# Another third PSUM bank, a batch begun one step sooner and merged operand sums in a fused attention and MLP kernel

## The chip, the cores and the metric

The kernel runs on one core of a Trainium2 chip. The metric is the device time of one execution in microseconds (us). A profiled execution also gives a span, from its first to its last instruction, and a trace of every instruction with its start and end. Engines are named as in the profile: PE (TensorE, matmuls), PEld (its weight loads), DVE (VectorE), ACT (ScalarE), POOL (GpSimd) and SP (SyncE); POOL and SP mostly issue DMAs here.

## The reference

Eight batches of grouped attention (16 query heads, 4 key and value heads, 384 tokens, head size 64) feed a residual MLP with affine scales in place of norms:

```python
scores = (1/sqrt(64)) * q @ k.T                     # per head; k, v shared by 4 query heads
x   = softmax(scores) @ v                           # heads side by side: [8, 384, 1024]
tok = einsum('ts,bsd->btd', w_tok, alpha1 * x + beta1)
u   = x + lam * tok
a2  = alpha2 * u + beta2
out = u + lam * (relu(a2 @ w_ch1) @ w_ch2)          # w_ch1 1024x4096, w_ch2 4096x1024
```

## The kernel before

**Stages.** Batches 0 and 1 are computed one by one (`main`). Batches 2 to 7 go through the MLP two at a time in three stages (`pair(0)`, `pair(1)`, `pair(2)`). A stage multiplies the two batches' stacked 2x2 block matrix by the blocks of the weights with a seven-product scheme in place of eight: sums and differences of blocks are formed on DVE, and seven products `o` are made and added up. The first product of a stage (first matmul by `w_ch1`, L723) runs over 8 groups `g` of 14 small products each, in the order of `SEQ1`; a small product is four matmuls of 128x384 into a bank X, Y or Z. The second product (second matmul by `w_ch2`, L785, tile C) runs over the seven `o` in the order 1, 2, 6, 5, 3, 7, 4 (`PLACE2`), and in each over three token tiles `ms` with 16 matmuls of 128x512.

**Steps.** Both products are generators. The second product yields after every four matmuls: 12 steps for each of the first six `o`, and 12 for `o` = 4, which is made in two halves `h` of eight matmuls for each `ms`. So it has steps 0 to 83; `o` = 7 has steps 60 to 71, `o` = 4 has 72 to 83, and its third token tile is first touched in step 76. A plan, written out by hand at the end of the kernel, holds functions under (stage, product, step); what stands under step u is issued right after the matmuls of step u. Every engine runs its instructions in this order.

**The work beside the second product.** In the first two of the three stages, the attention and token mixing of the next two batches, c and c+1, run in the gaps of the second product. `side(b)` returns a table of steps. Per batch it has six `scores3` (three score tiles each, L279, and three `exp` on ACT, L288; the last `exp` of some is put off until after the next value product), and for each of eight parts p (128 columns, two heads) a value product `av` (L315; then DVE divides by the row sums, L320 and L323, and makes the operand of the token product, L328 and L330) and a token product `tok` (L340; then DVE adds it to x, L347, and scales it, L351). `tok_flip` is `tok` and then a spill of x to `out` by DMA (L243) and a transposition by DMA (L362). For the parts 5, 6 and 7 of the second batch the transposition is made by PE in `turn` instead (L427) and copied out by ACT (L429). Batch c's table is used as it is, batch c+1's with 39 added to each step.

**PSUM.** `share_banks` gives out the eight banks anew for each product. In the second product two banks are `acc`, two buffers for C, and the other six are three score tiles of two banks each, sc0, sc1 and sc2. `three()` hands these out in rotation: scores, value products, token products and turns take one each, and each has to wait until the tile's last user is read out. The last product of a stage, `o` = 4, has three C tiles open at once in the first two of the three stages, since its two halves go over all `ms`: two in `acc`, the third in a score tile (`c_banks`). From then on `three()` skips that tile (`held`). In the last stage there are no score tiles in use, and C takes banks of them for its third token tile throughout and for the end of `o` = 7.

**DVE's other work there.** C is read out by L817, L819, L822 and L824 (the last for `o` = 7), and scaled by L687 (`scaled`, called by `flush` at certain steps) ahead of an accumulating store to `out` by POOL (L516). For the next stage DVE makes differences of weight blocks (`sum_w1`, L620 and L625), the operand sums of four parts (`sums_a`, three operations each, L585 to L587, of opb(0) to opb(5), planned at steps 74, 77, 80 and 82) and, in the next stage's first group, opb(6) (L740). The second small operand opb(0) is first used by the third small product (`o` = 7, bank Y), opb(6) by the tenth (`o` = 3, bank X).

**Weights.** A ring of six slots holds blocks of 512 KB; `load_w1` (POOL, L185) and `fetch` (SP, L636) fill a slot when the last step that reads it frees it. Two more slots lie in `pad`.

Of the kernel before, what the change touches and what calls it, by code (L numbers as in the profile page):

```python
# [12 lines left out]
def kernel(  # L13
# [22 lines left out]
    f32 = mybir.dt.float32  # L36
# [4 lines left out]
    ADD = mybir.AluOpType.add  # L41
# [7 lines left out]
    P = 128  # L49
# [145 lines left out]

    def three():
        if pairs:
            pairs["turn"] = (pairs["turn"] + 1 + (pairs["turn"] == 0 and pairs["held"])) % 3
            return pairs["sc%d" % pairs["turn"]].tile([P, 2, 4, P], f32, tag="sc", name="sc", bufs=1)
        return threes[0].tile([P, 2, 4, P], f32, tag="sc", name="sc", bufs=3)  # L200

# [27 lines left out]
    def side(b):  # L229
# [201 lines left out]
        if not first:  # L431


            turns = {}
            if b == 1:
                turns = {4: [(to_all, 3, 0, 0), (to_all, 3, 1, 1), (load_row_set, 1, 1, 0), (load_row_set, 2, 0, 1)],
                         8: [(k_transpose, 0)], 12: [(to_all, 1, 0, 2), (to_all, 1, 1, 0), (load_row_set, 2, 1, 0)],
                         16: [(scale_beta,)], 20: [(to_all, 2, 0, 1), (to_all, 2, 1, 0)],
                         24: [(q_transpose, 0, 2, "av")], 28: [(k_transpose, 2)]}
                for i in range(3):  # L440
                    turns[32 + 4 * i] = [(q_transpose, 2 + 2 * i, 2, "av")]
            if (b - NPL) // 2 > 0:
                at = {}

                def put(k, *m):
                    at.setdefault(k, []).append(m)

                for j in range(6):
                    put((0, 6, 12, 21, 26, 31)[j], scores3, j, j in (2, 5))
                for p in range(NP):  # L450
                    put((4, 10, 14, 18, 24, 29, 33, 35)[p], av, p)
                    put((8, 15, 17, 22, 27, 32, 36, 38)[p], tok_flip, p)
                    if by_pe(p):
                        put((36, 39, 41)[p - NP + 3], turn, p)
                return turns, at
            return turns, {
                0: [(scores3, 0)], 4: [(av, 0)], 6: [(scores3, 1)], 8: [(tok_flip, 0)], 11: [(av, 1)],
                13: [(scores3, 2, True)], 15: [(av, 2)], 16: [(tok_flip, 1)], 18: [(tok_flip, 2)], 19: [(av, 3)],
                21: [(scores3, 3)], 23: [(tok_flip, 3)], 25: [(av, 4)], 27: [(scores3, 4)], 29: [(tok_flip, 4)],
                31: [(av, 5)], 33: [(scores3, 5, True)], 35: [(av, 6), (tok_flip, 5)], 37: [(av, 7)],  # L460
                38: [(tok_flip, 6)], 41: [(tok_flip, 7)],
                **{39 + 4 * i - i // 2 * 2: [(turn, p)] for i, p in enumerate((5, 6, 7)) if by_pe(p)}}
# [118 lines left out]

    tt = nc.vector.tensor_tensor

    def sums_a(j):
        tt(out=opb(2)[:, j], in0=opb(0)[:, j], in1=opb(1)[:, j], op=ADD)  # L585
        tt(out=opb(0)[:, j], in0=opb(3)[:, j], in1=opb(0)[:, j], op=SUB)  # L586
        tt(out=opb(5)[:, j], in0=opb(2)[:, j], in1=opb(3)[:, j], op=SUB)  # L587

    kept, tb = {}, {}

# [79 lines left out]
    def pair(i):  # L670
# [82 lines left out]
                    tt(out=hid[:, ts, 3], in0=hid[:, ts, 2], in1=hid[:, ts, 1], op=ADD)  # L753
                yield 0
        finish(slice(NH - 2, NH))
        share_banks("acc", "sc1", "sc0", "sc2")
        acc = pairs["acc"]

        def c_banks(ms):
            return [(0, 512, pairs["sc1"].tile([P, 2, 512], f32, tag="sc", name="C", bufs=1)[:, 0] if ms == NST - 1 else  # L760
                     acc.tile([P, 512], f32, tag="acc", name="C", bufs=2))]

        X = [c_banks(ms) if last else None for ms in range(NST)]
# [2 lines left out]
        for k, o in enumerate(PLACE2):  # L766
            whole = not last and o != 4
            for h in range(1 if whole else 2):
                for ms in range(NST):
                    if o == 4 and not last and 1 < 3 * h + ms < 5:  # L770
                        sum_w1(0, (5, 7, 6)[3 * h + ms - 2])
                    if last and (o, h) in ((6, 1), (7, 0)):
                        (lift_end if o == 7 else begin_end)(ms)
                    if last and (o, h, ms) == (7, 0, NST - 1):
                        X[ms] = [(c0, c1, pairs[sc].tile([P, 2, 512], f32, tag="sc", name="C", bufs=1)[:, 0, :c1 - c0])
                                 for sc, c0, c1 in (("sc0", 0, 384), ("sc2", 384, 512))]
                    if whole:
                        X[ms] = [(0, 512, acc.tile([P, 512], f32, tag="acc", name="C", bufs=2))]
                    elif not last and h == 0:
                        X[ms] = c_banks(ms)  # L780
                        pairs["held"] = ms == NST - 1
                    upto = NH if whole else 8 * h + 8
                    for (c0, c1, x), t in ((c, t) for c in X[ms] for t in range(8 * h, upto)):
                        slot, rhs = w2_slots[i, 4 * k + t // 4], w2_at[i, 4 * k + t // 4]
                        nc.tensor.matmul(out=x, lhsT=hid[:, t, LEFT2[o], ms * P:(ms + 1) * P],  # L785
                                         rhs=rhs[:, t % 4 * 512 + c0:t % 4 * 512 + c1],
                                         start=((not last or o in (1, 6, 7)) and t == 0), stop=(t == NH - 1),
                                         skip_group_check=True)
                        if t % 4 == 3 and ms == NST - 1 and c1 == 512 and not (o == 4 and slot >= RING):
                            free(slot)  # L790
                        if last and o == 4 and t == NH - 1:
                            e, v = ends[ms][:, c0:c1], spare(ms).bitcast(f32)[:, c0:c1]
                            tt(out=v, in0=x, in1=lam_t[:, c0:c1], op=MUL)
                            tt(out=e, in0=e, in1=v, op=ADD)
                            nc.sync.dma_start(out=by_tok(out[b0 + 1])[:, ms, c0:c1], in_=e)
                        if t % 4 == 3 and t < upto - 1 and c1 == 512:
                            q = 4 * ms + t // 4
                            if whole and o in (2, 6) and q in (2, 5, 8, 10):
                                sums_hid(o, (2, 5, 8, 10).index(q))
                            if t % 8 == 3:  # L800
                                flush(1)
                            yield 1
                    if k == ms == h == 0:
                        pad_free[:] = [RING, RING + 1]
                        pump()
                    if (whole or h == 1) and not (last and o == 4):
                        if o in (1, 6, 5):
                            q = ((1, 6, 5).index(o) * NST + ms) * 512
                            snap[o, ms] = snaps[:, q:q + 512]
                        else:  # L810
                            bb, dw = where[o]
                            t = snap[1, ms] if o == 7 else spare(ms).bitcast(f32)
                        for c0, c1, x in X[ms]:
                            if o == 1:
                                nc.scalar.copy(out=snap[o, ms], in_=x)
                            elif o in (6, 5):
                                tt(out=snap[o, ms], in0=x, in1=snap[1 if last or o == 6 else 6, ms], op=ADD)  # L817
                            elif o == 2 and last:
                                tt(out=t, in0=x, in1=lam_t[:, :512], op=MUL)  # L819
                            else:  # L820
                                base = {2: 1, 3: 1 if last else 5, 7: 5, 4: 6}[o]
                                tt(out=t[:, c0:c1], in0=x, in1=snap[base, ms][:, c0:c1], op=ADD)  # L822
                            if o == 7 and not last:
                                tt(out=snap[6, ms], in0=x, in1=snap[6, ms], op=ADD)  # L824
                        if o not in (1, 6, 5):
                            later.append((scaled, o, b0 + bb, ms, dw, t))
                    if last and o in (2, 6) and (h, ms) in ((0, 1), (0, 2), (1, 0), (1, 1)):
                        sums_hid(o, [(0, 1), (0, 2), (1, 0), (1, 1)].index((h, ms)))
                    yield 1
# [4 lines left out]
    with tc.manual_schedule(engines=order):  # L834
# [162 lines left out]
        for i in range(NB - 1):  # L997
# [5 lines left out]
            put_all(ps, 1, side(c)[1])  # L1003
            for u, f, h in ((10, flip_q, 0), (17, flip_k, 0), (18, flip_q, 2), (28, flip_q, 4), (33, flip_k, 2), (33, flip_q, 6)):
                put(ps, 1, u, f, c + 1, h, 2)
            put_all(ps, 1, side(c + 1)[1], lambda u: u + 39)
            for j, u in ((1, 77), (0, 74), (2, 80), (3, 82)):
                put(ps, 1, u, sums_a, j)
        for ps in range(NPL + NB):
            done = [0, 0]  # L1010
            for second in main(ps) if ps < NPL else pair(ps - NPL):
# [43 lines left out]
```

## Time and profile before

| | us |
|---|---|
| median of 3 runs (747.96 to 750.38) | 748.25 |
| the profiled execution | 747.4 |
| its span | 745.6 |
| second product of the first paired stage | 316.60 to 419.68 |
| second product of the second paired stage | 492.83 to 595.91 |
| PE busy in each of these two (103.08 long) | 99.47 |
| DVE busy in the same | 77.65 and 77.43 |
| DMA engines' share in the same | 0.96 and 0.95 |

The times inside the span count from its first instruction. "Busy" is the union of an engine's instructions; the end of a matmul is modelled, so that a gap on PE is best counted from the start of one instruction to the start of the next. A name such as `xr<-sc,xr` is what an instruction writes and what it reads.

### The profile page before, as it was taken

The page shows a single profiled execution, that of the slowest core. Times are in us where ns is not written, and L with a number is a line of the kernel's source. Part 1 is how long each engine was busy: PE and PEld are TensorE (multiplying, and loading weights), DVE is VectorE, ACT ScalarE, POOL GpSimd, SP SyncE. Part 2 cuts the span into 40 slices and gives each one's busy share as a digit, 9 for nine tenths or more (in the row PEclk, how much of TensorE's full clock was granted, in tenths as well). Part 3 has the DMA queues.
Part 4 walks back from the last instruction along what each step waited for, and adds up shares of the span by engine and source line. Part 5 has one row for each costly group of instructions (what it writes and reads, how often), then busy time and mean ns, then how long its engine had stood idle before and what let it go on. Part 6 is the DMA issues. An engine that isn't in the chain of part 4 may idle for free.

```text
span 745.6 us, 14462 instructions
## 1 busy us (share of the span) xinstructions
PE 728.5 (98%) x5710; PEld 418.7 (56%) x5769; DVE 522.2 (70%) x1010; ACT 319.1 (43%) x458; POOL 163.2 (22%) x211
## 2 busy tenths in 40 slices
PE   8999999999999999999999899999999899999997
PEld 5856555566555566655555466655555456654444
DVE  7763366577677899749778977747958887762344
ACT  7622341433342666653334366663343266660000
POOL 9434220420000232301021433110002231000011
PEclk9999999999999999999999999999999999999999
DMA  9999999999998999998979999999979998936975
GB/s 185 193 201 200 207 216 165 182 190 203 212 275 244 187 219 211 250 258 201 275 191 246 151 195 173 195 195 206 269 232 185 195 181 114 154 120 235 285 216 102
DMA packets 218017, 151.32 MB, mean 203 GB/s; under 512 B 88660, under 2 KB 197060, under 8 KB 217948
## 3 DMA queue, kind: packets, MB, share of 16 engines
q0 software_dynamic: 120304, 64.60, 65.9%
q1 hardware_dynamic: 97100, 85.39, 41.8%
q8 instruction: 45, 0.74, 0.4%
q10 hardware_dynamic: 544, 0.39, 0.2%
q14 instruction: 24, 0.20, 0.1%
HBM read 154.84 MB, written 38.27 MB: 259 GB/s over the span
## 4 chain that ended last, share of the span: by engine, by line
PE 85%; DVE 7%; DMA 4%; issue 2%; POOL 1%; ACT 0%; DVEq 0%
PE C L785 25%; PE X L723 16%; PE ch L569 10%; PE h L531 10%; PE Y L723 8%; PE sc L279 4%; PE Z L723 4%; PE sc L315 3%; PE sc L340 3%; DMA q_raw<-in_q_dram 2%; DMA ops<-a 1%; DVE xr L323 1%; DVE a1f L328 1%; DVE xr L347 1%; DVE hT L822 1%
## 5 line engine op out<-in xcount | busy, mean ns | idle before, releaser
L288 ACT ACTIVATE es<-sc 128x1024 bf16<-128x1024 f32 x126 | 121.4, 1023 | 163.8 <-PE sc L279 152.6
L785 PE MATMUL C<-w,arena 128*128 128x512 bf16 (+2 forms) x777 | 179.8, 373 | 6.8 <-DVE xr L347 5.0
L785 PEld LDWEIGHTS <-arena 128*128 128x128 bf16 x1040 | 94.8, 98 | 105.7 <-issue 10.3
L728 ACT ACTIVATE hT<-X,bias 128x384 f32<-128x384 f32 x144 | 83.7, 582 | 61.0 <-PE X L723 53.8
L723 PEld LDWEIGHTS <-w 128*128 128x128 bf16 x768 | 75.2, 98 | 50.0
L185 POOL DMA_DIRECT2D w<-in_moe_w_ch_dram x68 | 61.4, 911 | 131.7 <-PE X L723 73.8
L569 PE MATMUL ch<-arena,hT 128*128 128x512 bf16 x366 | 87.9, 379 | 1.0 <-issue 0.3
L516 POOL DMA_DIRECT2D out_dram<-hT x33 | 28.5, 863 | 260.6 <-DVE hT L687 161.1
L531 PE MATMUL h<-ops,w 128*128 128x384 bf16 (+1 forms) x480 | 83.3, 327 | 1.6 <-DVE hT L542 1.4
L723 PEld LDWEIGHTS <-pad 128*128 128x128 bf16 x576 | 56.3, 98 | 38.0 <-issue 0.8
L723 PE MATMUL X<-ops,w 128*128 128x384 bf16 x384 | 70.3, 326 | 0.0
L723 PE MATMUL X<-ops,pad 128*128 128x384 bf16 x384 | 70.3, 326 | 0.0
L531 PEld LDWEIGHTS <-w 128*128 128x128 bf16 x480 | 45.4, 98 | 31.2 <-issue 2.4
L569 PEld LDWEIGHTS <-hT 128*128 128x128 bf16 x384 | 34.8, 98 | 36.8 <-issue 2.5
L785 PE MATMUL C<-pad,arena 128*128 128x512 bf16 (+2 forms) x222 | 52.0, 372 | 0.1
L347 DVE TENSOR_TENSOR xr<-sc,xr 128x384 f32<-128x384 f32 x56 | 30.9, 552 | 21.3 <-PE sc L340 21.3
L315 PEld LDWEIGHTS <-es 128*128 128x128 bf16 x1008 | 38.3, 97 | 12.4
L340 PEld LDWEIGHTS <-wtokT 128*128 128x128 bf16 x576 | 37.4, 98 | 12.3 <-DVE a L330 1.8
L279 PE MATMUL sc<-qT,kT 64*128 64x384 bf16 (+2 forms) x576 | 41.7, 272 | 1.6 <-ACT hT L288 0.2
L315 PE MATMUL sc<-v,es 128*128 128x65 bf16 x1008 | 39.9, 193 | 0.0
L723 PE MATMUL Y<-ops,w 128*128 128x384 bf16 x192 | 39.4, 326 | 0.4 <-DVE ops L586 0.4
L320 DVE RECIPROCAL rinv<-sc 128x6 f32<-128x6 f32 x56 | 10.7, 191 | 40.6 <-PE sc L315 40.5
(138 smaller groups left out, 910.6 us busy)
## 6 DMA issues: line engine op xcount, KB each, us to landing
w<-in_moe_w_ch_dram POOLq DMA_DIRECT2D x68, 512.0 KB, 10.5
w<-w2s SPq DMA_DIRECT2D x66, 512.0 KB, 4.5
out_dram<-xr SPq DMA_DIRECT2D x56, 192.0 KB, 6.5
pad<-w2s SPq DMA_DIRECT2D x18, 512.0 KB, 8.1
out_dram<-hT POOLq DMA_DIRECT2D x33, 256.0 KB, 6.9
arena<-in_moe_w_ch_dram POOLq DMA_DIRECT2D x16, 512.0 KB, 19.7
w2s<-arena SPq DMA_DIRECT2D x28, 256.0 KB, 3.9
q_raw<-in_q_dram POOLq DMA_DIRECT2D x28, 192.0 KB, 11.2
```

What stands on the lines that cost most here:

```text
L185: nc.gpsimd.dma_start(out=w1[:, w1_slots[c]], in_=w1src[:, :, c * CW * P:(c + 1) * CW * P])
L279: nc.tensor.matmul(out=sc[:, hh, k % 4:k % 4 + n], lhsT=kT[r, 2 * p // G, BLK[hh][sk], :], rhs=qT[r, p, st:st + n, :], start=True, stop=True)
L288: nc.scalar.activation(out=e, in_=sc, func=EXP, scale=scale_qk)
L315: nc.tensor.matmul(out=av[:, hh, sq, :], lhsT=ess[k // 4][:, m % 2, k % 4, :], rhs=vb[:, sk, hk, :], start=(sk == 0), stop=(sk == NST - 1))
L340: nc.tensor.matmul(out=ps[:, tt, :], lhsT=wtokT[:, st, tt * P:(tt + 1) * P], rhs=a1s[p][:, st, :], start=(st == 0), stop=(st == NST - 1 an ...
L347: nc.vector.tensor_tensor(out=u, in0=ps, in1=u, op=ADD)
L516: nc.gpsimd.dma_start(out=at, in_=o, accum_op=ADD)
L531: nc.tensor.matmul(out=ps[:, :n], lhsT=w1[:, w1_slots[c], dt, j * P:(j + 1) * P], rhs=a2T[:, dt, :n], start=(dt == 0), stop=(dt == NDT - 1))
L569: nc.tensor.matmul(out=ps, lhsT=hT[:, nt, ms * P:(ms + 1) * P], rhs=w2[:, row(nt)[0], row(nt)[1], cs], start=(i == 0), stop=(i == NNT - 1))
L723: nc.tensor.matmul(out=ps, lhsT=tb[g, o][:, dt, e * P:(e + 1) * P], rhs=opb(LEFT1[o])[:, dt], start=(o in (1, 2, 7) and dt == 0), stop=(dt ...
L728: nc.scalar.activation(out=snap[o, e], in_=ps, func=IDENT, bias=hi if o == 5 else lo)
L785: nc.tensor.matmul(out=x, lhsT=hid[:, t, LEFT2[o], ms * P:(ms + 1) * P], rhs=rhs[:, t % 4 * 512 + c0:t % 4 * 512 + c1], start=((not last o ...
```

## The change

It has three parts.

- The third C bank of `o` = 4 is taken from sc0 in place of sc1, so `three()` skips sc0 while it is held. The order in which the pools are opened has sc0 in sc1's place, and the last stage's uses of sc1 and sc0 are exchanged.
- The second batch's table is used with 38 added to each step in place of 39; the last token product of the first batch moves from step 38 to 39.
- The operand sums of parts 0 and 1 are made together at step 76, in operations of twice the size; those of parts 2 and 3 move from 80 and 82 to 79 and 81. Before, part 0 was at step 74 and part 1 at 77.

```diff
@@ def three():
-            pairs["turn"] = (pairs["turn"] + 1 + (pairs["turn"] == 0 and pairs["held"])) % 3
+            pairs["turn"] = (pairs["turn"] + 1 + (pairs["turn"] == 2 and pairs["held"])) % 3
@@ def side(b):
-                    put((8, 15, 17, 22, 27, 32, 36, 38)[p], tok_flip, p)
+                    put((8, 15, 17, 22, 27, 32, 36, 38 if b % 2 else 39)[p], tok_flip, p)
@@
-    def sums_a(j):
-        tt(out=opb(2)[:, j], in0=opb(0)[:, j], in1=opb(1)[:, j], op=ADD)
-        tt(out=opb(0)[:, j], in0=opb(3)[:, j], in1=opb(0)[:, j], op=SUB)
-        tt(out=opb(5)[:, j], in0=opb(2)[:, j], in1=opb(3)[:, j], op=SUB)
+    def sums_a(j, n=1):
+        js = slice(j, j + n)
+        tt(out=opb(2)[:, js], in0=opb(0)[:, js], in1=opb(1)[:, js], op=ADD)
+        tt(out=opb(0)[:, js], in0=opb(3)[:, js], in1=opb(0)[:, js], op=SUB)
+        tt(out=opb(5)[:, js], in0=opb(2)[:, js], in1=opb(3)[:, js], op=SUB)
@@ def pair(i):
-        share_banks("acc", "sc1", "sc0", "sc2")
+        share_banks("acc", "sc0", "sc1", "sc2")
-            return [(0, 512, pairs["sc1"].tile([P, 2, 512], f32, tag="sc", name="C", bufs=1)[:, 0] if ms == NST - 1 else
+            return [(0, 512, pairs["sc0"].tile([P, 2, 512], f32, tag="sc", name="C", bufs=1)[:, 0] if ms == NST - 1 else
-                                 for sc, c0, c1 in (("sc0", 0, 384), ("sc2", 384, 512))]
+                                 for sc, c0, c1 in (("sc1", 0, 384), ("sc2", 384, 512))]
@@ the plan
-            put_all(ps, 1, side(c + 1)[1], lambda u: u + 39)
-            for j, u in ((1, 77), (0, 74), (2, 80), (3, 82)):
-                put(ps, 1, u, sums_a, j)
+            put_all(ps, 1, side(c + 1)[1], lambda u: u + 38)
+            for j, u in ((0, 76), (2, 79), (3, 81)):
+                put(ps, 1, u, sums_a, j, 1 if j else 2)
```

## The prediction

> **What bounds the kernel now.** I read the page first: TensorE (PE) is busy 98% of the 745.6 us span, its granted clock is 0.999, and the chain that ended last is mostly its own work.
>
> ```profile
> PE 728.5 (98%) x5710; PEld 418.7 (56%) x5769; DVE 522.2 (70%) x1010; ACT 319.1 (43%) x458; POOL 163.2 (22%) x211
> ...
> PE 85%; DVE 7%; DMA 4%; issue 2%; POOL 1%; ACT 0%; DVEq 0%
> ```
>
> So only a moment in which PE stands still can give time back. The view of PE's waits lists them: the instruction that waited, the releaser, total us, times, longest.
>
> ```profile
> PE C L785 <- DVE xr L347: 5.0, 2, 2.5
> ...
> PE Y L723 <- DVE ops L586: 0.4, 2, 0.2
> ```
>
> The first line is two stalls of the second product (C). Then I read the timeline of PE and VectorE (DVE) around the first; columns are start, duration, then the instruction.
>
> ```profile
> 408.63 0.33 PE L427 MATMUL sc<-ident,obuf 128*128 128x128 bf16 x3
> 408.80 0.67 PE L340 MATMUL sc<-a,wtokT 128*128 128x128 bf16 x9
> 411.94 1.89 PE L785 MATMUL C<-w,arena 128*128 128x512 bf16 x8 [2.48 <-DVE xr L347]
> ...
> 409.93 0.56 DVE L330 TENSOR_TENSOR a<-a1f,vecs 128x384 bf16<-128x384 f32 x1
> 410.40 0.35 DVE L585 TENSOR_TENSOR ops<-ops 128x384 bf16<-128x384 bf16 x1
> 410.79 0.36 DVE L586 TENSOR_TENSOR ops<-ops 128x384 bf16<-128x384 bf16 x1
> 411.07 0.35 DVE L587 TENSOR_TENSOR ops<-ops 128x384 bf16<-128x384 bf16 x1
> 411.34 0.55 DVE L347 TENSOR_TENSOR xr<-sc,xr 128x384 f32<-128x384 f32 x1
> ```
>
> The reader is to see this: the token product of part 6 (L340, second line) wrote a score tile; the third C bank is that very tile, and DVE reads it only at 411.34, behind its backlog. Stage two shows the same lines 176.23 us later, to 0.01 us. I count steps from these starts: four C matmuls take 0.86 us, twelve score matmuls 0.76 (0.10 more ahead of them after a C step), a pair's 18 value matmuls 0.55, a token product 0.50, a turn 0.17. By that C could have started at 409.30; the stall is 2.64 us in starts (2.48 on record, which counts from a modelled end).
>
> **The third bank (tile sc1 to sc0).** 68 score tiles are asked for before the bank is taken, before and after the change, in a rotation of three. Call 67 (token product 6) has sc1, call 66 (the turn of part 5) has sc0. So the bank now waits for ScalarE's copy of turn 5. That copy starts 0.37 after its turn and takes 0.48 (409.00); after it come token product 6 and step 75, 1.36 us. It is done 0.5 us early, and ScalarE has nothing else there (idle 2.47 before it). The stall goes: **-2.64** per stage. The skip in the rotation moves with the bank, so the two tiles asked for while it is held are again one sc2, the other plain tile, and sc2. The swapped names in the pool list put sc0 where sc1 was; in the last stage, which has no batch beside it, nothing else changes: 0.
>
> **The second batch one step sooner, token product 7 of the first batch one step later.** Nothing is added: scores, value products, token products, turns, their spills (SP) and transposes (SP) all go past one C step (0.86 us), and SP's last two weight fetches (400.67, 401.30) stand behind one transpose as before. At step 38 PE waited 0.21 us for token product 7: step 38 ends at 363.36, the product starts at 363.57 when DVE's L330 (362.96 + 0.56) is done. Now the scores come first and the product follows a step later: **-0.21**. The third score tile there needs DVE's L347 of product 6, due 0.06 late: I count 0. In each of the other seven parts three to five C steps lie between value and token product (2.6 us or more) against 1.9 us of DVE work and at most 1.3 us of eviction; I found no new wait but the tail.
>
> **What is late next: DVE's queue in the tail.** I laid DVE's program out in its new order, with start-to-start times of before (L347 0.59, L351 0.48; L320, L323, L328, L330 together 1.88; L822, L824, L620, L625, L687 0.60 each, an L687 right behind its L822 0.72 later; the three sums 0.93). It becomes continuous from token product 5 (DVE at 403.21) to the seam. Merging two parts' sums makes 3 operations of 128x768 out of 6. That form is in the trace, at 0.56 us against 0.35; so 1.55 for 1.86, **0.31 us of DVE** saved, none of it PE's own.
>
> ```profile
> 318.07 0.56 DVE L753 TENSOR_TENSOR arena<-arena 128x768 bf16<-128x768 bf16 x1
> ...
> 414.37 0.56 DVE L347 TENSOR_TENSOR xr<-sc,xr 128x384 f32<-128x384 f32 x1 [1.29 <-PE sc L340]
> ...
> 421.82 0.32 PE L723 MATMUL Y<-ops,w 128*128 128x384 bf16 x1 [0.19 <-DVE ops L586]
> ...
> 424.49 0.95 DVE L740 TENSOR_TENSOR ops<-ops 128x1536 bf16<-128x1536 bf16 x1
> ```
>
> Step by step after the change: product 7 wants its operand at 409.96, and DVE ends it at 409.91 plus some 0.05: no wait, no margin. The next stage's first X matmul comes at 416.85 (419.68 before: 2.64 + 0.21 sooner, rounded). The Y matmul that needs the last sum then waits 0.21 us (it waited 0.35 before, counted in starts). L740, whose result the tenth small product (L723, o=3) needs, ends at 423.08, and that product wants it at 422.91: a **new wait of 0.22**. Before, it ran at 425.88 with L740 done at 425.44. After: 423.13. Per stage 425.88 - 423.13 = **2.75 us**, in two stages **5.5 us**.
>
> [...]
>
> **Weights at the seam.** DVE's sum L625 right before L740 needs a weight block that POOL asks for when step 77 is done: issued 414.18, landed 422.75, used 423.88 (stage two: 590.40, 600.17, used 600.25). After: asked at 411.3, wanted at 421.5; with the 8.6 and 9.8 us of before it is there by 419.9 and 421.1. Two blocks later, POOL's load stands behind a store that DVE releases, now 3.7 us after the stage's start (2.3 before); by the same 10.8 us it lands 14.5 after it (13.1 before). DVE's later work for that group may slip 1.44 us before PE meets it at the Y banks (0.78 us of room at L736, 0.66 of idle DVE). I take 0.
>
> [...]
>
> **The sum.** The profiled execution took 747.4 us (span 745.6 and 1.8 around it): 747.4 - 5.5 = 741.9. The median of the runs shown is 748.25, so 0.85 above; taken from it, **742.8**.
>
> **Rivals.**
> *Late fetch in a stage, 744.4.* The last weight fetch of stage two was issued at 577.51 and landed 590.35 (12.8 us), while packets around 581 took up to 3.5 us. Its first use (step 79) was after 591.4, behind the stall; it moves to 588.6. That is a wait of 1.76, less some 0.15 that the tail then saves: +1.6. Against: in stage one the same bytes were there 2.4 us before the new use.
> *DVE is the bound of the tail, 745.9.* If the 1.29 us gap of before (the row at 414.37) is not closed and the merge saves nothing, DVE ends 1.6 us later per stage: 748.25 - 2 x 1.15. For it: no gap is left in my layout.
> *Weight landings do not move, 746.5.* If the block lands at 422.75 and 600.17 regardless, L625 holds L740 up by 1.28 and 2.47 us: gains of 1.47 and 0.28. For it: DMA is 0.95 busy over these stages; against it: it idled in the stall.
> *The stall only changes its name, 747.8.* The third bank finds its tile held by something that the rotation hides from me; 0.2 per stage remains from step 38.
> *Slower, 753.9.* The load two blocks on becomes the bound of the first product: if it takes 16.4 us from issue, the longest landing of that line, it comes 20.1 after the stage's start, PE stops 5.6 us at the Y banks, and two stages lose 2 x (5.6 - 2.75). It decides from a landing 17.3 us after the start, 13.6 after issue; against it: 10.8 and 10.4 there now.
>
> **Chances.** Forecast 0.56; late fetch 0.15; DVE 0.08; landings 0.09; same stall 0.06; slower 0.06. The range 741.5 to 746.0 holds the first three, with 1.3 below for a tail without new waits (0.43 a stage) and the scatter of the runs. A change under 0.3% (2.2 us) can't be told from none: faster (below 746.0) 0.79, same 0.15, slower 0.06.
>
> **What would show it.** The wait C <- L347 is gone and none under C replaces it; ScalarE's copy of turn 5 ends some 0.5 us before the third bank; seam to seam the stage is 2.6 to 2.9 us shorter; DVE has no gap over the last 18 us; a wait of X on L740 near 0.2 appears. I am wrong if C waits for a DMA near step 79, or if X waits for L740 by more than 1 us.

## The result and the profile after

The changed kernel takes 743.26 us (median of 6 runs, 741.59 to 743.98) against 748.35 us of the kernel before (6 runs). The ratio is 0.9926, with a 95% interval of 0.9911 to 0.9942: 0.74% faster. Run again beside other kernels it gave 742.72 us and a ratio of 0.9912 (0.9898 to 0.9926). The forecast was 742.8.

The profiled execution has a span of 741.0 us (745.6 before). First the view of PE's waits of the changed kernel, the lines that fall in the paired stages: the two stalls of C behind L347 are gone, and nothing under C has taken their place (the 0.2 us under `C <- issue` stands where the record of a matmul of step 77 is missing). New are X behind L741 (L740 of the kernel before) and Y behind L737.

```profile
...
PE X L724 <- DVE ops L741: 0.8, 2, 0.5
PE C L786 <- issue: 0.3, 2, 0.2
...
PE Y L724 <- DVE arena L737: 0.3, 1, 0.3
```

PE's timeline around the old stall of the first paired stage: token product 6 (L340 at 407.08) is followed at once by C, and C's third bank is taken in the middle of the row of 8 matmuls.

```profile
406.91 0.33 PE L427 MATMUL sc<-ident,obuf 128*128 128x128 bf16 x3
407.08 0.67 PE L340 MATMUL sc<-a,wtokT 128*128 128x128 bf16 x9
407.58 1.89 PE L786 MATMUL C<-w,arena 128*128 128x512 bf16 x8
409.32 0.66 PE L340 MATMUL sc<-a,wtokT 128*128 128x128 bf16 x9
...
416.20 1.46 PE L724 MATMUL X<-ops,w 128*128 128x384 bf16 x8
...
422.66 1.48 PE L724 MATMUL X<-ops,w 128*128 128x384 bf16 x8 [0.26 <-DVE ops L741]
```

The bank now waits for ScalarE's copy of the turn of part 5:

```profile
407.28 0.48 ACT L429 COPY ops<-sc 128x384 bf16<-128x384 bf16 x1 [2.47 <-PE sc L427]
```

The copy ends at 407.76, and C wants the bank at 408.45, the fifth start of its row. DVE's timeline shows the seam, where the new wait comes from: no idle note from token product 5 on (402.56, the first row here) until the second L626, which starts 0.20 later than its place in the queue.

```profile
402.56 0.56 DVE L347 TENSOR_TENSOR xr<-sc,xr 128x384 f32<-128x384 f32 x1 [0.73 <-PE sc L340]
...
411.91 0.55 DVE L586 TENSOR_TENSOR ops<-ops 128x768 bf16<-128x768 bf16 x1
412.50 0.56 DVE L587 TENSOR_TENSOR ops<-ops 128x768 bf16<-128x768 bf16 x1
412.98 0.55 DVE L588 TENSOR_TENSOR ops<-ops 128x768 bf16<-128x768 bf16 x1
...
420.24 0.68 DVE L626 TENSOR_TENSOR pad<-w,pad 128x1024 bf16<-128x1024 bf16 x1
421.04 0.69 DVE L626 TENSOR_TENSOR pad<-w 128x1024 bf16<-128x1024 bf16 x1
421.65 0.95 DVE L741 TENSOR_TENSOR ops<-ops 128x1536 bf16<-128x1536 bf16 x1
```

To compare kernels I cut the trace at the first C and the first X matmul of each paired stage. An unbroken first product takes 72.80 us, as the first of the three shows in every profile. A first product behind a seam is late by what PE waited: for the last operand sum (third small product), for L741 (tenth), and for the Y banks that L731 and L737 read out (in groups 1 and 2). The last column is when the weight block that the second L626 needs had landed, after the seam. Two numbers are the two stages.

| kernel | second product | first product after it | late: last sum | L741 | Y banks | block landed |
|---|---|---|---|---|---|---|
| before | 103.08, 103.08 | 73.15, 73.15 | 0.35, 0.35 | 0, 0 | 0, 0 | 3.1, 4.3 |
| before, once more | 103.11, 104.77 | 73.15, 73.15 | 0.35, 0.36 | 0, 0 | 0, 0 | 3.1, 3.2 |
| changed | 100.39, 100.42 | 74.11, 73.69 | 0.18, 0.18 | 0.43, 0.70 | 0.69, 0 | 4.8, 5.0 |
| changed, once more | 100.39, 100.57 | 74.67, 73.87 | 0.19, 0 | 1.68, 1.04 | 0, 0 | 6.1, 5.2 |
| bank alone | 100.70, 100.67 | 74.19, 74.19 | 1.39, 1.39 | 0, 0 | 0, 0 | 4.1, 4.8 |
| all but the bank | 101.72, 101.73 | 72.80, 73.61 | 0, 0 | 0, 0 | 0, 0.83 | 2.9, 3.9 |
| sums not merged | 100.40, 100.41 | 73.75, 73.53 | 0.51, 0.51 | 0.44, 0.21 | 0, 0 | 5.2, 4.8 |
| product 7 at 38 | 100.94, 100.94 | 73.59, 74.02 | 0.18, 0.18 | 0.60, 1.02 | 0, 0 | 5.0, 5.4 |
| scalings carried | 100.39, 100.38 | 73.99, 73.93 | 0, 0 | 1.18, 1.11 | 0, 0 | 5.4, 5.3 |
| loads before stores | 100.39, 100.40 | 74.22, 74.39 | 0.19, 0.18 | 1.22, 1.41 | 0, 0 | 5.6, 5.7 |
| begin at 37 | 101.63, 101.62 | 72.80, 73.05 | 0, 0 | 0, 0 | 0, 0.25 | 4.0, 3.6 |
| L741 first | 100.40, 100.41 | 73.95, 73.57 | 0.18, 0.18 | 0, 0 | 0.99, 0.60 | 5.8, 5.4 |
| L741 first and carried | 100.39, 100.39 | 72.80, 72.80 | 0, 0 | 0, 0 | 0, 0 | 4.6, 4.9 |

Between the first profiles of the two kernels the four stretches sum to 352.46 and 348.61 us: 3.85 us are gone in the paired stages, 5.35 off the second products and 1.50 given back after the seams. The rest of the spans' difference (4.66) is 0.79 ahead of the first paired stage, where the change alters nothing. The medians differ by 5.1, more than either; experiments 9 and 10 show why.

### The profile page after: what moved, and what is told of

Its sections match the earlier page's. It is cut to its first block, busy times and chain, and to the rows that moved or that the text cites. A ratio compares the mean times of both kernels' runs of the same rounds, so it can differ in the third digit from the quotient of the medians.

```text
span 741.0 us, 14454 instructions
## 1 busy us (share of the span) xinstructions
PE 727.3 (98%) x5710; PEld 418.0 (56%) x5769; DVE 521.7 (70%) x1004; ACT 319.5 (43%) x458; POOL 163.4 (22%) x211
## 4 chain that ended last, share of the span: by engine, by line
PE 81%; DMA 7%; DVE 5%; issue 4%; POOL 3%; POOLq 0%; DVEq 0%
PE C L786 24%; PE X L724 15%; PE ch L569 10%; PE h L531 10%; PE Y L724 8%; PE sc L279 4%; PE Z L724 4%; PE sc L315 3%; DMA w<-in_moe_w_ch_dram 3%; PE sc L340 3%; DMA q_raw<-in_q_dram 2%; DMA ops<-a 1%; POOL w L185 1%; DVE xr L323 1%; DMA rows<-in_moe_lam_dram 1%
## 5 line engine op out<-in xcount | busy, mean ns | idle before, releaser
L347 DVE TENSOR_TENSOR xr<-sc,xr 128x384 f32<-128x384 f32 x56 | 30.9, 553 | 22.8 <-PE sc L340 22.8
L340 PEld LDWEIGHTS <-wtokT 128*128 128x128 bf16 x576 | 37.5, 98 | 11.8 <-DVE a L330 0.8
L320 DVE RECIPROCAL rinv<-sc 128x6 f32<-128x6 f32 x56 | 10.8, 192 | 42.5 <-PE sc L315 42.3
## 6 DMA issues: line engine op xcount, KB each, us to landing
w<-in_moe_w_ch_dram POOLq DMA_DIRECT2D x68, 512.0 KB, 10.4
```

The source lines that it names most:

```text
L340: nc.tensor.matmul(out=ps[:, tt, :], lhsT=wtokT[:, st, tt * P:(tt + 1) * P], rhs=a1s[p][:, st, :], start=(st == 0), stop=(st == NST - 1 an ...
L347: nc.vector.tensor_tensor(out=u, in0=ps, in1=u, op=ADD)
```

## The experiments

The theory: the stall was one wait for a tile, its removal is worth nearly its length, and then DVE's queue in the tail of a stage is what PE meets. The rivals: PE alone bounds it, so that either edit brings it all; or the weights at the seam bound it.

**1. The bank alone**, on the kernel before.

```diff
-            pairs["turn"] = (pairs["turn"] + 1 + (pairs["turn"] == 0 and pairs["held"])) % 3
+            pairs["turn"] = (pairs["turn"] + 1 + (pairs["turn"] == 2 and pairs["held"])) % 3
...
-        share_banks("acc", "sc1", "sc0", "sc2")
+        share_banks("acc", "sc0", "sc1", "sc2")
...                                                # and sc0 for sc1 in c_banks, sc1 for sc0 in the last stage
```

> The kernel before with the third C bank from sc0 alone; steps and sums as before. Theory (the stall was one wait; without it DVE's queue bounds the tail): the wait C <- L347 of 2.64 us in starts shrinks to about 0.2, for ScalarE's copy of turn 5 ends at 409.48 and C wants the bank at 409.30; the second product goes from 103.08 to about 100.7 in each stage. DVE starts token product 7's L347 only 1.36 earlier (its gap of 1.29 closes), so the Y matmul at the seam waits about 1.4 us for the last sum (L586) where it waited 0.35. Gain some 1.4 us a stage, 745.6 in all. Rival (PE is the bound, DVE only trails): the whole 2.4 us a stage stays, no wait over 0.4 at the seam, 743.4. Rival (the wait only changes its name): over 2 us under another name inside the second product, 748.

Measured: 743.99 us, ratio 0.9935 (0.9920 to 0.9951). PE's waits in its profile:

```profile
PE Y L723 <- DVE ops L586: 2.5, 2, 1.2
```

The second product went to 100.70 and 100.67 and the wait for the last sum to 1.39 us, as laid out. So the stages gained 2.71 us where the stall had cost 5.28: DVE's queue is the bound behind the stall. By the median the gain is 4.85, not the 2.7 expected; that surplus is the one of the whole change too (9 and 10).

**2. All but the bank**: the changed kernel with the third bank from sc1.

```diff
-            pairs["turn"] = (pairs["turn"] + 1 + (pairs["turn"] == 2 and pairs["held"])) % 3
+            pairs["turn"] = (pairs["turn"] + 1 + (pairs["turn"] == 0 and pairs["held"])) % 3
...                                                # and sc1 and sc0 exchanged in the other three places
```

> The changed kernel with the third C bank from sc1 again; 38 steps, product 7 and merged sums as changed. Theory: the wait C <- L347 is back, but at 1.3 us a stage in place of 2.64, since the sums no longer stand ahead of that L347 on DVE (it ends at 409.74 in the changed kernel's time, C wants the bank at 408.45). The second product takes about 101.7. But PE's waits at the seam (Y for the last sum, X for L741, Y banks after the late weight block) go, as PE comes later: the first product about 73.0 in place of 74.11 and 73.69. In all 0.3 to 0.8 a stage slower than the changed kernel: 743.9 to 744.9. Rival (the bank is the change, the shift is decoration): 747 or more.

Measured: 743.31 us, ratio 0.9930 (0.9914 to 0.9946), under the 743.9 to 744.9 expected.

```profile
PE C L786 <- DVE xr L347: 2.4, 2, 1.2
...
PE Y L724 <- DVE arena L737: 0.3, 1, 0.3
```

The stall came back at half its length (second product 101.72), and the waits at the seam went in stage one, but stage two met the Y banks (0.83). The stages sum to 349.86, 1.25 more than the changed kernel's first profile and 0.36 more than its second. So either edit alone takes 2.6 to 2.7 us out of the stages, and both together 3.0 to 3.85: they remove the same stall, and the bank beside the other two parts is worth 0.4 to 1.25 us, which the medians can't tell (743.31 and 743.26).

**3. Sums not merged**: six operations of 128x384 at step 76.

```diff
-            for j, u in ((0, 76), (2, 79), (3, 81)):
-                put(ps, 1, u, sums_a, j, 1 if j else 2)
+            for j, u in ((0, 76), (1, 76), (2, 79), (3, 81)):
+                put(ps, 1, u, sums_a, j)
```

> The changed kernel with the operand sums of parts 0 and 1 as six operations of 128x384 at step 76 in place of three of 128x768. Theory A (DVE's own queue is what X waits for at L741): DVE needs 0.31 us more ahead of L741, and the wait X <- L741 grows by 0.31 in both stages (0.43 to 0.74, 0.70 to 1.0, in starts against before). Theory B (in stage two the weight block that lands late is what holds L741): in stage one, where DVE stood 0.12 for the block, 0.2 more; in stage two, where it stood 0.40, nothing more. Both: 0.2 to 0.6 us in all.

Measured: 742.23 us in one run. Both theories missed. The 0.31 us of DVE shows as 0.33 at the last sum (0.18 to 0.51 in both stages, one wait that I had not named), but X waited less for L741, and the first product was even shorter. L741 starts 5.79 and 5.56 us after the seam. In stage one DVE stood for the block (landed at 5.2); in stage two the block (4.8) was there, and DVE's queue, 0.33 longer, set the start. In the changed kernel (5.45 and 5.72, blocks at 4.8 and 5.0) DVE stood for the block in both. What the merge saves is real and smaller than what the landing of one block varies.

**4. Product 7 at step 38 again.**

```diff
-                    put((8, 15, 17, 22, 27, 32, 36, 38 if b % 2 else 39)[p], tok_flip, p)
+                    put((8, 15, 17, 22, 27, 32, 36, 38)[p], tok_flip, p)
```

> The changed kernel with the first batch's last token product at step 38 again, ahead of the second batch's scores. Theory: PE waits 0.21 us there for DVE's L330 in each of the two stages, and DVE's tail, which hangs on PE at token product 5, comes 0.21 later with it: second product 100.6 in place of 100.4, first product as in the changed kernel, 0.4 us in all. Rival (the wait was never there, or the swap adds one of its own at the third score tile): 100.4 or less.

Measured: 743.80 us in one run; second product 100.94, which is 0.55 over the changed kernel, not 0.2. PE's timeline in the order of this kernel: the token product starts 0.22 late for its operand, and the scores, now right behind it, wait for DVE's L347 of that product.

```profile
361.87 1.03 PE L786 MATMUL C<-pad,arena 128*128 128x512 bf16 x4
362.95 0.68 PE L340 MATMUL sc<-a,wtokT 128*128 128x128 bf16 x9
363.56 0.61 PE L279 MATMUL sc<-qT,kT 64*128 64x384 bf16 x8
364.47 0.40 PE L279 MATMUL sc<-qT,kT 64*128 64x128 bf16 x4 [0.31 <-DVE xr L347]
```

So with the second batch a step sooner, the exchange of the two is what keeps that shift from costing 0.5 us a stage.

**5. The scalings carried on**: the last three L688 with their stores in groups 1 to 3 of the next stage.

```diff
-                            if t % 8 == 3:         # in the second product
+                            if t % 8 == 3 and (last or o != 4 or h == 0):
...
-        flush()                                    # at the end of a stage
+        if last:
+            flush()
+        carried.extend(later)
...
+                if k == 12 and g and carried:      # in the next stage's first product
+                    f, *a = carried.pop(0)
+                    f(*a)
```

> The changed kernel in which the last three scalings L688 of a paired stage's second product (o=4), with their stores, are carried into groups 1 to 3 of the next stage's first product. DVE has 1.85 us less ahead of L741, and POOL asks for the two later weight blocks (now 1.6 and 3.7 us after the seam) without the stores ahead of them, some 2 to 3 us sooner. Theory DVE queue (L741 is late because DVE is busy): X waits no more for L741, both stages of the first product go to about 72.8: 2.2 us off the two. Theory landing (L626, right ahead of L741, waits for the weight block that lands 4.8 to 5.0 us after the seam): X2 and X6 stay late by 0.6 to 0.9 together, and only the Y bank waits of stage one (0.69) go: 73.4 to 73.7 in both.

Measured: 742.67 us in one run. DVE's timeline of this kernel (L742 is L741):

```profile
418.13 0.68 DVE L626 TENSOR_TENSOR pad<-w,pad 128x1024 bf16<-128x1024 bf16 x1
421.44 0.69 DVE L626 TENSOR_TENSOR pad<-w 128x1024 bf16<-128x1024 bf16 x1 [2.63 <-DMA w<-in_moe_w_ch_dram]
422.05 0.95 DVE L742 TENSOR_TENSOR ops<-ops 128x1536 bf16<-128x1536 bf16 x1
```

DVE has the time, stands 2.63 us idle for the block, and L742 is no sooner (6.0 us after the seam): the theory of the landing holds, the one of DVE's queue falls for L741. The wait for the last sum went with the queue. X was late by 1.18 and 1.11, more than expected, for the block landed 5.4 and 5.3 us after the seam. The two later loads were asked for 2.0 and 3.2 us sooner here (1.9 and 2.9 in stage two), while it was in flight.

**6. Loads before stores**, DVE's program untouched.

```diff
-            store(b, ms, dw, t)
+            if o == 4 and not last:
+                behind.append((b, ms, dw, t))
+            else:
+                store(b, ms, dw, t)
...
         flush()
+        for a in behind:                           # after the last step's loads
+            store(*a)
```

> The changed kernel with the three stores of o=4 asked for after the step's weight loads, DVE's program untouched. POOL asks for the two later weight blocks some 2 to 3 us sooner. Theory landing two blocks on: they land before PE needs the Y banks, the waits Y <- L737 of stage one (0.22 and 0.47) are gone, the wait X <- L741 stays or grows by up to 0.3 as the block in flight shares the queue: first product 73.4 to 73.8 in both stages. Rival (these waits are DVE's backlog, not the block): stage one stays at 74.1.

Measured: 744.52 us in one run. There is no wait for the Y banks in either stage, as the later blocks landed 10.9 and 11.3 us after the seam (15.7 and 14.3 in the changed kernel). But the block in flight landed at 5.6 and 5.7, and X waited 1.22 and 1.41 for L741: in all 0.1 and 0.7 worse. That the sooner loads slowed it is not shown: experiment 9 asks for them at the same points, and its block landed at 4.6 and 4.9.

**7. Begin at 37.**

```diff
-            put_all(ps, 1, side(c + 1)[1], lambda u: u + 38)
-            for j, u in ((0, 76), (2, 79), (3, 81)):
+            put_all(ps, 1, side(c + 1)[1], lambda u: u + 37)
+            for j, u in ((0, 75), (2, 78), (3, 80)):
```

> The changed kernel with the second batch one more step sooner: 37 added to its table, its sums at 75, 78 and 80. DVE's tail hangs on PE at token product 5 and comes 0.86 us sooner against the seam. Theory landing: the wait Y for the last sum (0.18) goes, but L741 stays at 5.5 us or more after the seam behind the block that L626 waits for, so X is late by the same 0.6 to 0.9 in all; the Y bank waits of stage one go or shrink: 100.4 and 73.4 to 73.8. Theory DVE queue: X6 goes on time too, 72.8 to 73.0. Rival: an operand is not ready where one step less lies between, and the second product grows past 100.5.

Measured: 743.47 us in one run, and the rival is right about the second product, 101.63:

```profile
PE sc L279 <- DVE xr L347: 1.7, 2, 0.8
...
PE sc L340 <- DVE a L330: 0.4, 2, 0.2
```

The scores at step 37 wait 0.8 us a stage for a tile that DVE's L347 holds, and a token product 0.2 for its operand. The seam is free of DVE's queue (L741 at 4.62), as laid out. What is gained at the seam is lost earlier.

**8. L741 first**: the operand difference ahead of the weight difference of group 1.

```diff
-                if k in (2, 5, 8, 11) and g + 1 < NH // 2:
-                    sum_w1(g + 1, {2: 5, 5: 7, 8: 6, 11: 4}[k])
+                if k in (2 if g or not i else 3, 5, 8, 11) and g + 1 < NH // 2:
+                    sum_w1(g + 1, {2: 5, 3: 5, 5: 7, 8: 6, 11: 4}[k])
```

> The changed kernel with L741 (opb(6)) ahead of the weight difference L626 of group 1 in DVE's program at a paired stage's start, nothing else moved. Theory landing: L741 no longer stands behind a wait for a weight block and is done some 5.6 us after the seam, X6 is on time; X2 is late by 0.18 as before. Since PE then comes sooner, the Y banks may be waited for by up to 1.0 in stage one: first product 73.0 to 74.0 in stage one and 73.0 in stage two (74.11 and 73.69 in the changed kernel). Theory DVE queue: L741 gains only the 0.6 of one L626.

Measured: 742.49 us in one run. L741 starts 4.64 us after the seam and X waits for it no more, in either stage, though the block landed late (5.8 and 5.4). PE then met the Y banks, 0.99 and 0.60: in stage one as expected, in stage two, where I expected nothing, because the later block landed at 15.2 there (14.3 in the changed kernel).

**9. Both, the changed kernel again and the kernel before again.** Edits 5 and 8 together make the version that the experiments point to.

> The changed kernel with both edits: L741 ahead of the weight difference L626 of group 1, and the last three scalings L688 with their stores carried into groups 1 to 3 of the next stage. Theory landing: X waits neither for DVE's backlog nor for the block; the later blocks land some 10.6 us after the seam and the Y banks are free in time; second product 100.4, first product 72.8 to 72.9 in both stages, 2.1 us off the two stages of the changed kernel, 741.2 by its median. Rival (PE then meets the next wait: L626 stands for the block until 5.4 us after the seam and the group's Y reads come late): Y waits of 0.2 to 0.7 a stage, 742 to 743.

> The changed kernel once more, beside the others on the same chip: 743.3, second product 100.4 in both stages; the first product between 73.5 and 74.4, as the blocks land.

> The kernel before once more, with a second profile. Its median lies 0.9 us over its profiled execution, and the two profiles differ by 3.85 us in the paired stages where the medians differ by 5.1. Theory (the rest is scatter ahead of the paired stages): again 103.08 and 73.15 in both stages, and another start of the first paired stage, 243 to 245. Rival (the stages themselves vary): a first product after the seam over 73.5.

Measured: the version with both edits takes **740.60 us** (4 runs, 739.93 to 741.29), ratio to before 0.9882 (0.9868 to 0.9896); the changed kernel beside it 742.72. Its second products are 100.39 and its first products 72.80, an unbroken row. DVE still waits for the block, but behind L742:

```profile
418.79 0.95 DVE L742 TENSOR_TENSOR ops<-ops 128x1536 bf16<-128x1536 bf16 x1
420.72 0.69 DVE L626 TENSOR_TENSOR pad<-w 128x1024 bf16<-128x1024 bf16 x1 [0.97 <-DMA w<-in_moe_w_ch_dram]
```

The changed kernel's second profile has X 1.68 and 1.04 late for L741, with the block at 6.1 and 5.2: its first products scatter with DMA between 73.7 and 74.7. The second profile of the kernel before brought what I had not looked for. Its first second product starts no later (316.03), but its second paired stage is 1.69 us longer. The view of busy time by stretches of it, with the granted clock (PEclk) as the last column but two:

```profile
580.00:588.00 8.00, 5.47 (x65) 3.45 (x65) 7.69 (x18) 1.57 (x3) 0.84 (x1) 1.00 1.10 254
588.00:591.40 3.40, 3.40 (x15) 1.61 (x13) 0.78 (x2) 0.00 (x0) 1.10 (x2) 0.50 0.57 121
591.40:597.00 5.60, 5.55 (x34) 2.83 (x33) 5.15 (x12) 0.96 (x2) 1.19 (x2) 1.00 1.28 158
```

And PE's timeline there: C comes out of the stall at 587.64, its 8 matmuls take until 590.70 where they took 1.72 before.

```profile
587.64 3.27 PE L785 MATMUL C<-w,arena 128*128 128x512 bf16 x8 [2.48 <-DVE xr L347]
590.70 1.00 PE L340 MATMUL sc<-a,wtokT 128*128 128x128 bf16 x9
```

So my theory of a scatter ahead of the stages fell. The stall had a second price in this execution: 3.4 us at a clock of 0.50 behind it, and 1.69 us lost by it.

**10. The stall filled**: the kernel before with 13 unused matmuls inside the stall.

```diff
+            if b % 2 and b > NPL + 1 and p == NP - 2:
+                for _ in range(13):
+                    nc.tensor.matmul(out=whole[:, 1, :NST].rearrange("p a b -> p (a b)"), lhsT=wtokT[:, 0, :P],
+                                     rhs=wtokT[:, 1, :], start=True, stop=True)
```

> The kernel before, with 13 more matmuls of 128x384 (2.1 us by the 0.1625 us of a row of that form) right behind token product 6 of the second batch, into the half of its score tile that nothing reads; their results are used nowhere. They lie inside the stall of 2.64 us, which keeps its end: second product 103.1 in both stages. The one thing changed is that PE is idle for about 0.5 us there and not 2.6. Theory clock (the kernel before loses 1.7 us in such an execution and stage as the granted clock falls to 0.5 for 3.4 us after the stall, seen in the second profile of before, and its mean clock of 0.993 to 0.998 in most executions is that): mean clock 0.999 to 1.0 in all executions, median 747.0 to 747.6, ratio to before 0.997 to 0.998. Rival (the scatter of before has another source, its mean clock is a by-product): median as before, 748.4 to 749.3, clock 0.995 to 0.998 in most executions.

Measured: **747.08 us** (12 runs), ratio 0.9975 (0.9962 to 0.9988) to the 748.97 of the kernel before beside it. The mean granted clock was 0.999 or 1.0 in 11 of its 12 executions; beside it the kernel before had 0.993 to 0.998 in 16 of 17. In its profile C still waits (L352 is L347), and its second products are even longer, 103.38:

```profile
408.14 2.28 PE L349 MATMUL sc<-wtokT 128*128 128x384 bf16 x13
411.07 1.89 PE L790 MATMUL C<-w,arena 128*128 128x512 bf16 x7 [0.65 <-DVE xr L352]
```

Work that nobody reads made the kernel 1.9 us faster. That settles the clock as the other part of the stall's price.

## Why the prediction was right, and where it was not

**The stall goes: right.** The third bank waits for nothing. The layout had the copy of turn 5 done 0.5 us early; it was 0.7. The second product lost 2.69 and 2.66 us where the steps gave 2.83 (2.64 and 0.21, rounded).

**The exchange at step 38: right in sign, two small misses.** The wait of 0.21 went, but the third score tile waits about 0.15 for L347 of product 6, which I had due at 0.06 and counted as 0 (the twelve score matmuls take 0.91, not 0.76). That is the missing 0.14. Experiment 4 puts the price of not exchanging at 0.55, more than the 0.21 that I counted.

**DVE's tail: right to a few hundredths.** Measured from the seam, token product 5's L347 stood at -13.64 as laid out, the first L626 at +4.04 (4.07 laid out), and the last sum made PE wait 0.18 (0.21). Experiment 1 is the same layout with another order, 1.39 for 1.4.

**The weights at the seam: the step that failed.** I took the landing times of before, 8.6 and 9.8 us after asking, an asking that moves with the seam, and a cost of 0. The asking moved less: token product 7 (0.50 us) stood behind step 77 before and stands ahead of it now, so the block is asked for 5.05 us ahead of the seam, not 5.51. That alone uses up the room of stage two (421.1 in the layout, wanted at 421.5). In the changed kernel the block then took 9.9 and 10.1 us, 11.1 and 10.4 in the second profile, and X waited for L741 0.43 and 0.70, then 1.68 and 1.04, in place of 0.22. The later block took 12.0 us in stage one, not 10.8, and landed 15.73 after the seam; less the 0.61 by which PE was late already that is 15.1, over the 14.5 from which I had PE meet the Y banks: 0.69 us. The other profiles bear that point out (a wait of 0.83 at 15.2 with PE on time, none at 14.3). So the mechanisms were the ones that I had put among the rivals, and they belonged in the sum: beyond the 0.22 a stage they cost 1.4 us over both stages in the first profile and 2.3 in the second.

**What the sum lacked: the clock.** I priced the stall at its length. In experiment 9 one stage with it lost 1.69 us more, where the clock fell to 0.50 for 3.4 us; in experiment 10 filling it brought 1.9 us by the medians. In 42 executions of the kernel before whose mean clock is listed, 3 have 0.999 (median 746.7 us), 18 have 0.997 or 0.998 (748.3) and 21 have 0.993 to 0.995 (749.65 for the 17 with 0.995). One stretch of 3.4 us at 0.5 takes 1.7 / 748 = 0.0023 off the mean, so as an estimate these are executions with none, one and two or more such stretches (the profile that shows one has 0.997). The profile that I worked from had none (its clock is 1.00 in the 3.4 us behind both stalls), and by this estimate that is why it lay 0.95 below the median; I noted that gap and did not ask for its cause.

So it is luck that the measured 743.26 lies so near to 742.8. The gain is 5.35 from the second products (I had 5.66), less 1.5 to 2.2 given back at the seams (I had 0.16), and, by the estimate above, one or two stretches of 1.7 from the clock in most executions (I had 0); the last two errors offset each other. The signs that I had named show it: from the first X matmul of a stage to the next stage's, the two are 2.69 and 1.70 us shorter than in the first profile of before, 2.69 and 0.99 in the second profile, where I had 2.6 to 2.9. X waited for L741 by more than 1 us, which was to show me wrong, in the second profile and not in the first. **Of the rivals**, the late fetch did not come (C waits for no DMA); DVE as the bound is true of the bank alone; the weight landings moved, but less than PE did.

Not settled: why the blocks land later, and why the same order of loads landed between 4.8 and 6.1 in the changed kernel. One thing goes with it: where the second product takes 101.6 us or more (before, all but the bank, begin at 37, the stall filled) the block took 7.9 to 9.8 us from asking to landing, where it takes 100.4 to 100.9, 9.6 to 11.1. No run tests whether that is the cause.

## What to carry to other kernels

When a stall goes, lay out the next queue to the end of the stage in the new order, and price each transfer by the spread of its line's landings, not by the one beside it: here 17.7 us of DVE's queue came out within 0.03 us, and a block landed 0.8 to 3.0 us later against the seam than laid out. Two edits that remove one stall don't add up; each alone may bring most of it. An operation that only needs what is on chip should not stand behind one that waits for a transfer in an engine's order: moving one such line, and three scalings with their stores, brought another 2.1 us. And before working from a profile, set its mean granted clock beside that of the other executions: the one used here was one of 3 in 42 with 0.999.

## What the runs showed of the hardware

A stall of 2.5 us on PE can cost more than its length. In one of four stalls of that kind (2.48 us each) in two profiles the granted clock fell to 0.50 for 3.4 us right after it, and the 8 matmuls of C behind it took 3.06 us where they took 1.72 (1.69 us lost in that stage). Two facts say that it is the idleness: with 13 matmuls in the stall (idle 0.65 in place of 2.48) the mean clock was 0.999 or more in 11 of 12 executions, and in the kernel without the bank change, with stalls of 1.2 us, in 6 of 6; the kernel before had 0.993 to 0.998 in 39 of 42.

In the first profile of before, the same stall, from 585.69 to 588.17, left the clock at 1.00:

```profile
580.00:588.00 8.00, 5.64 (x72) 3.69 (x71) 7.72 (x17) 2.11 (x3) 0.84 (x1) 1.00 1.16 201
588.00:591.40 3.40, 3.17 (x23) 1.80 (x24) 2.04 (x5) 0.00 (x0) 1.82 (x2) 1.00 0.97 238
```

Why the clock fell behind one of the four stalls and not behind the others is not shown.
